# Threshold attention and a SoLU feed-forward block in one kernel: the second tile's first product moved up two rounds

## The chip, the cores and the metric

The kernel runs on one core of a Trainium2 chip. Its engines work in parallel, each through its own list of instructions in order: TensorE (PE) multiplies, VectorE (DVE), ScalarE (ACT) and GpSimd (POOL) do the elementwise work, and SyncE (SP) issues nearly all transfers. A transfer that has to wait for something is waited for by the SP queue, and what stands behind it in that queue waits too. The metric is the device time of one execution in microseconds, as the median of several.

## The reference

Attention over 8 batches of 8 heads, 576 positions, 64 elements a head, all in float32:

```
scores = q @ k.T / 8
thresh = max(scores) - tau            # per row, tau = 0.02
scores = where(scores >= thresh, scores, -1e9)
attn   = exp(scores - max(scores));  attn /= sum(attn) + 1e-9
x      = attn @ v                     # then (B, H, S, D) -> (B*S, H*D): 4608 x 512
h      = x @ w_in                     # 512 x 1024
s      = h * softmax(h)
ln     = (s - mean(s)) / sqrt(var(s) + 1e-6) * g_ln
out    = ln @ w_out                   # 1024 x 512
```

The weights `w_in` and `w_out` come as 64-bit floats, and the kernel turns them into 32-bit ones itself.

## The kernel before

**Rounds.** The attention is cut into 144 slots, 18 to a batch, and the main loop (L893) runs one slot a round. A slot is one block of 128 query rows for two heads: `scores` (L457) multiplies q by k into two PSUM tiles, `maxes` (L490) takes the row maximum on VectorE, `ramp` and `exps` (L514, L521) do threshold and exponential on ScalarE, `normalise` (L529) scales the rows on GpSimd one round later, and `blocks` (L539) turns the result into `T` on VectorE. After every second slot `blocks` also issues three transfers (L556, L558; four at L563 for the odd slots of the last rows), which move `T` into `wT`. There are two `wT` buffers, so a unit's transfer may start only when the unit two before it has been multiplied by v.

**Product with v.** `attend_steps` (L567) multiplies `wT` by v, and `attended` (L600) copies the result to `xh`, the input of the feed-forward block. When a unit is due (`pv_due`, L807), it is multiplied in the first round whose other work allows it: before the change in a round with no feed-forward step or with an h step, not beside an o step (L976).

**Feed-forward.** A tile is 128 tokens. Its product with `w_in` is two steps, h0 and h1 (L633), its product with `w_out` two steps, o0 and o1 (L751), one step a round. Between them, with h1 in round r: maximum and exponential at the end of r, product with h in r+1, statistics in r+2, normalisation on ScalarE and VectorE and the transfer `ff_swap` (L731) in r+3, the transpose `ff_turn` (L741) to `uT` at the end of r+4, and o0 can read `uT` in r+5. The variable `quarter` counts h0, h1, o0, o1; the o steps between h1 and the next h0 are those of the tile before. For the first tile there is none before, so rounds 13 and 14 have no feed-forward step (L1006 does nothing).

**Transposes and weights in the early rounds.** The q and k of the second batch are transposed on TensorE beside the scores of rounds 13 to 21 (`preps`, L813); one of these pieces, `e_item` (L413), transposes the last 64 positions of q and k, which `load_ends` (L140) brings in behind the main loads of round 9 (k) and round 11 (q). In rounds 0 to 15 each round also converts one piece of the weights (L277 to L334). Later batches are transposed on VectorE (`turn_natural`, L210), scaled on GpSimd (L197).

**SP's order.** In a round SP gets `ff_swap` first (middle jobs), then the `wT` transfers, then the store of a finished tile, then the transfers of transposed q and k, then loads (`load_at`), then those of the weights. All transfers of SP share eight completion semaphores in turn.

Work on TensorE by round, besides scores in each; "t" counts transposed pieces of q and k, a unit in brackets is (batch, kind, head pair), a tile (batch, kind, half). Starts are those of the first matmul of a round in the trace of before.

```
round  start us   before                             after
12      72.5      h1(000) v(0,1,0)                   the same
13      80.8      -                                  t5 h0(001)
14      84.6      t5                                 t4 h1(001) v(0,1,1)
15      90.8      t7 h0(001) v(0,1,1)                -
16     100.6      t6 h1(001) v(0,1,2)                t5 v(0,1,2)
17     108.8      o0(000)                            t4 o0(000)
18     113.3      o1(000)                            o1(000) v(0,1,3)
19     117.7      t5 v(0,1,3)                        t5 h0(010)
20     122.9      t7 h0(010)                         t7 h1(010)
21     128.3      t6 h1(010) v(0,2,0)                t6 o0(001)
22     135.3      o0(001)                            o1(001)
23     141.8      o1(001)                            h0(011) v(0,2,0)
24     146.2      h0(011) v(1,0,0)                   h1(011) v(1,0,0)
25     152.6      h1(011) v(1,0,1)                   o0(010)
26     158.9      o0(010)                            o1(010)
27     163.4      o1(010)                            v(1,0,1)
28     167.8      v(1,0,2)                           v(1,0,2)
29     170.7      v(1,0,3)                           v(1,0,3)
30     174.2      h0(100)                            h0(100)
```

From round 30 to the end, both kernels do the same in the same rounds, with the two PSUM buffers p0 and p1 exchanged.

Of the kernel before, what the change touches and what calls it, by code (L numbers as in the profile page):

```python
# [8 lines left out]
F32 = mybir.dt.float32  # L9
# [7 lines left out]
P = 128  # L17
# [3 lines left out]
def kernel(  # L21
# [29 lines left out]
    DM, DFF = w_in.shape  # L51
# [13 lines left out]
    work = ctx.enter_context(tc.tile_pool(name="work", bufs=2))  # L65
# [35 lines left out]
    pairs_free = ["p0", "p1"]  # L101
# [6 lines left out]
    def fence(first):  # L108
        m = nc.gpsimd.memset(mark, 0.0)
        for mm in first:  # L110
            sync(m, mm)
        return m
# [37 lines left out]
    def load_v(b, hf, parts=(0, 1, 2)):  # L150
        d = halves.setdefault((b, hf), {})
        hs = slice(4 * hf, 4 * hf + 4)

        if b > 1:
            if 0 in parts:
                d["v"] = loads.tile([P, 4, NK, D], F32, tag="v", bufs=3, name="v")
            to = d["v"].rearrange("p h m d -> p h (m d)")
            rows = v_rows[64 * (H * b + 4 * hf) :][0:256]
            for part in parts:
                nc.sync.dma_start(**(  # L160
                    dict(
                        out=to.rearrange("p (e o) n -> p o e n", o=2)[:, 0],
                        in_=rows.rearrange("(e r) n -> r e n", e=2),
                    ),
                    dict(out=to[:, 1], in_=rows[64:192]),
                    dict(out=to[ROWS[1], 3], in_=rows[0:64]),
                    dict(out=to[ROWS[0], 3], in_=rows[192:256]),
                )[part])
            return
        if 0 in parts:  # L170
            d["v"] = loads.tile([P, 4, NK, D], F32, tag="v", bufs=3, name="v")
        rest = v[b, hs, 0:SM, :].rearrange("h (p t) d -> p h (t d)", t=4)
        for part, to, rows, of in (
            (0, 0, slice(0, P), slice(0, P)), (1, 4, ROWS[0], ROWS[1]), (1, 4, ROWS[1], ROWS[0])
        ):
            if part in parts:
                nc.sync.dma_start(
                    out=d["v"][rows, :, to : to + 4].rearrange("p h t d -> p h (t d)"),
                    in_=rest[of],
                )  # L180
        for rows in ROWS if 2 in parts else ():
            nc.sync.dma_start(
                out=d["v"][rows, :, NK - 1], in_=v[b, hs, SM:S, :].rearrange("h p d -> p h d")
            )
# [7 lines left out]
    def load_natural(i, nm, a):  # L192
        raw = loads.tile([P, 4, 4, D], F32, tag=nm, name=nm)
        natural[i, nm, a] = raw = raw.rearrange("p h t d -> p (h t d)")[:, 0 : NK * D]
        nc.sync.dma_start(out=raw, in_=qk_rows[nm][a, 64 * i : 64 * i + P])
# [437 lines left out]
    def ff_h(t, part, split, beside=()):  # L633
# [29 lines left out]
        if part == 0:  # L663
            d["fence"] = fence(last[-4:])

    def ff_max(t):
        d = ffn[t]
        d["nm"] = small.tile([P, 1], F32, tag="hm", name="hm")
        nc.vector.tensor_reduce(out=d["nm"], in_=d["h"], axis=AX.X, op=ALU.max, negate=True)  # L669

    def ff_exp(t):
        d = ffn[t]

        starts.append(t)
        tag = "xh1" if rnd > NS and len(starts) % 2 else "u"
        d["u"] = work.tile([P, DFF], F32, tag=tag, bufs=1, name="u")
        d["se"] = small.tile([P, 1], F32, tag="se", name="se")
        nc.scalar.activation(  # L678
            out=d["u"], in_=d["h"], func=AF.Exp, bias=d["nm"], scale=1.0, accum_out=d["se"]
        )  # L680
# [34 lines left out]
    def ff_norm(t):  # L715
        d = ffn[t]
        rs, nb = d["norm"]
        d["V"] = V = work.tile([P, 2, DFF // 2], F32, tag="V", bufs=1, name="V")
        u = d["u"].rearrange("p (g n) -> p g n", g=2)
        nc.scalar.activation(out=V, in_=u, func=AF.Identity, bias=nb, scale=rs)  # L720

# [19 lines left out]
    def ff_turn(t, rnd):  # L741
        d = ffn[t]
        turns.append(t)
        tag = "xh0" if rnd > NS and len(turns) % 2 else "uT"
        d["uT"] = uT = work.tile([P, 2 * NC, 2, 32], F32, tag=tag, bufs=1, name="uT")
        nc.vector.transpose(  # L746
            out=uT, in_=d["V"].rearrange("p y (m x) -> p m y x", x=32)
        )
        d["turned"] = rnd + 1
# [50 lines left out]
    NS = len(slots)  # L800
    PER = NS // B
# [12 lines left out]
    for i in range(NP, 2 * NP):  # L814
        at = (13, 15, 19, 20)[i - NP]
# [7 lines left out]
    load_at = {}  # L823
    scale_at, turn_at, ends_at = {}, {}, {}
    for at, job, hf, what in (
        (11, load_one, 0, "q"),
        (9, load_one, 0, "k"),
        (13, load_one, 1, "k"),
        (15, load_one, 1, "q"),
        (17, load_v, 0, (0,)),  # L830
        (19, load_v, 0, (1, 2)),
        (PER + 3, load_v, 1, (0,)),
        (PER + 5, load_v, 1, (1, 2)),
    ):
        load_at.setdefault(at, []).append(lambda job=job, hf=hf, what=what: job(1, hf, what))
    for i in range(2 * NP, NPAIR, 2):
        b, hf = divmod(i // 2, 2)
        ats = ((-5, -3), (-1, 1)) if hf else ((-13, -11), (-9, -7))
        if b == 2:
            ats = ((-3, -2), (-1, 1)) if hf else ((-13, -11), (-9, -5))  # L840
        for nm, pieces_at in zip("qk", ats):
            for a, at in enumerate(pieces_at):
                at += PER * b
                load_at.setdefault(at - 3 if b == 2 else (at - 3) // 4 * 4, []).append(
                    lambda i=i, nm=nm, a=a: load_natural(i, nm, a)
                )
                turn_at[at] = i, nm, a
                if nm == "q":
                    scale_at[at - 1] = i, a
        for j in range(2):  # L850
            ends_at[PER * b + ats[0][1] + 4 + j] = i + j
        if hf:
            v_ats = (2, 5, 5, 6) if b % 2 else (3, 4, 4, 7)
        elif b == 2:
            v_ats = -9, -7, -5, -3
        else:
            v_ats = (-11, -7, -3, -3) if b % 2 else (-9, -5, -1, -1)
        for part, at in enumerate(v_ats):
            load_at.setdefault(PER * b + at, []).append(
                lambda b=b, hf=hf, part=part: load_v(b, hf, (part,))  # L860
            )

    with tc.manual_schedule():
# [20 lines left out]
        ready = []  # L884
        rnd = 0
        prev = cur = None

        between, starts, turns = [], [], []
        quarter = 0
        w2_done = False  # L890

        begin, middle, late, norms = {}, {}, {}, {}
        while True:  # L893
# [8 lines left out]
            if rnd in norms:  # L902
                ff_norm(norms.pop(rnd))
            if rnd == NS:
                pairs_free += ["s0", "s1"]
                if prev is not None:
                    between.append(prev)
                    prev = None
                if quarter == 2:
                    between.append(cur)  # L910
                    cur = None
                    quarter = 0
                assert quarter != 3
            if (
                cur is None and quarter == 0 and ready and ready[0][0] <= rnd
                and (more or len(between) < 3 + (len(ready[0][1][0]) == 1))
            ):
                cur = ready[0][1].pop(0)
                if not ready[0][1]:
                    ready.pop(0)  # L920
            busy = cur is not None or prev is not None
            items = []
            if rnd - 1 in pieces:
# [37 lines left out]
            due = bool(pv_due) and pv_due[0][0] <= rnd  # L961
            step = None
            if quarter < 2 and cur is not None:
                step = ("h", quarter)
            elif quarter == 3:
                step = ("o", 1)
            elif not more:
                if between and ffn[between[0]].get("turned", NS + rnd) <= rnd:
                    prev = between.pop(0)
                    step = ("o", 0)  # L970
            elif quarter == 2 or (prev is not None and not due):
                if prev is None or (ffn[prev].get("turned", NS + rnd) <= rnd and w2_done):
                    step = ("o", 0)

            attending = None
            if due and (step is None or step[0] == "h") and len(pairs_free) > (step == ("h", 0)):  # L976
                attending = pv_due.pop(0)[1]
            beside = ()
            if attending is not None and attending[1] == 2 and step is not None:
# [1 line left out]
            if step == ("h", 0):  # L981
                ff_h(cur, 0, rnd + 1 < NS, beside)
                quarter = 1
            elif step == ("h", 1):
                ff_h(cur, 1, None, beside)
                quarter = 2
                late.setdefault(rnd, []).append(lambda t=cur: (ff_max(t), ff_exp(t)))
                late.setdefault(rnd + 1, []).append(lambda t=cur: (ff_mul(t), ff_sum(t)))
                middle.setdefault(rnd + 2, []).append(lambda t=cur: ff_stats(t))
                if rnd + 6 < NS:  # L990
                    norms[rnd + 3] = cur
                else:
                    late.setdefault(rnd + 2, []).append(lambda t=cur: ff_norm(t))
                middle.setdefault(rnd + 3, []).append(lambda t=cur: (ff_norm2(t), ff_swap(t)))

                at = rnd + 4 if more or not ready or len(ready[0][1][0]) == 1 else rnd + 6
# [4 lines left out]
                if not more:  # L1001
                    between.append(cur)
                    cur = None
                    quarter = 0
            elif step == ("o", 0):
                if prev is not None:  # L1006
                    ff_o(prev, 0)
                quarter = 3
            elif step == ("o", 1):
# [5 lines left out]
                prev, cur = cur, None  # L1015
                quarter = 0
            if attending is not None:
# [3 lines left out]
                b, kind, hp = attending  # L1021
# [25 lines left out]
            if rnd - 1 in pieces:  # L1047
                weight_d(pieces[rnd - 1])
                w2_done = pieces[rnd - 1] == NW - 1
# [34 lines left out]
```

## Time and profile before

| | before |
|---|---|
| median of three runs | 866.25 us (864.14 to 867.25) |
| profiled execution, its own time | 866.93 us |
| span of its trace | 865.1 us |
| TensorE busy | 820.7 us (95%) |
| VectorE busy | 682.1 us (79%) |
| ScalarE busy | 574.1 us (66%) |
| GpSimd busy | 497.0 us (57%) |
| round 13 to the start of round 30 | 80.8 to 174.2 us |

The own time of the profiled execution is 1.8 us over its span, and 0.7 us over the median. The table of slices in the profile cuts the span into 40 stretches of 21.6 us and gives each engine's busy share in tenths. A wait is put down to the instruction whose signal came last. "L479" is line 479 of the kernel before; in the kernel after, lines behind the first edit stand a few lines lower.

### The profile page before, as it was taken

Reading aid. Unit: us, or ns where it says so; the run is one execution under the profiler, and the core shown is the slowest. Engines: PE = TensorE matmul, PEld = TensorE weight load, DVE = VectorE, ACT = ScalarE, POOL = GpSimd, SP = SyncE. Lnnn points to the kernel's source line nnn. Section 1 sums busy time; section 2 is a strip of 40 time slices with the busy share of each in tenths; the row PEclk is TensorE's granted clock in tenths of the full one; section 3 lists DMA queues with packets and bytes.
Section 4 is the critical chain, followed back from the end, with each engine's and each line's share of the span. In section 5 each row is a group of like instructions: output and inputs, shape, how many; then the busy total and the mean of one; then the engine's idle time right before and its main releaser. Section 6 shows DMA issues by size and latency. Waiting matters only on the chain.

```text
span 865.1 us, 36118 instructions
## 1 busy us (share of the span) xinstructions
PE 820.7 (95%) x15361; PEld 626.8 (72%) x15361; DVE 682.1 (79%) x1248; ACT 574.1 (66%) x1153; POOL 497.0 (57%) x938
## 2 busy tenths in 40 slices
PE   5667899999999999999999999999999999999997
PEld 3345576776688887777788886777788888887655
DVE  5989778888788878888878887888888888787361
ACT  5867776676667776777677776777677776776121
POOL 2867656657656656565656656565666655555120
PEclk9879899999999999999999999999999999999999
DMA  7999978888879888888888787888788887655312
GB/s 234 254 242 252 231 167 210 210 234 205 224 174 227 210 184 214 213 213 206 197 210 228 199 191 195 219 220 208 188 224 228 196 195 184 153 142 140 69 38 62
DMA packets 83712, 168.54 MB, mean 195 GB/s; under 512 B 15448, under 2 KB 45152, under 8 KB 83552
## 3 DMA queue, kind: packets, MB, share of 16 engines
q1 hardware_dynamic: 82416, 164.25, 76.9%
q8 instruction: 120, 1.97, 1.0%
q10 hardware_dynamic: 1136, 2.00, 0.7%
q14 instruction: 40, 0.33, 0.1%
HBM read 46.14 MB, written 9.44 MB: 64 GB/s over the span
## 4 chain that ended last, share of the span: by engine, by line
PE 82%; DMA 6%; ACT 4%; DVE 3%; issue 2%; POOL 2%; SPq 1%; ACTq 0%; DVEq 0%; POOLq 0%
PE o_ps L759 26%; PE h_ps L654 22%; PE s_ps L479 15%; PE pv L589 14%; PE h_ps L644 3%; DMA wT<-T 2%; ACT w L516 1%; DVE w L501 1%; DMA raw<-in_moe_w_out_dram 1%; ACT w L525 1%; DMA q<-in_q_dram 1%; DMA raw<-in_moe_w_in_dram 1%; DVE T L547 1%; PE s_ps L344 1%; POOL w L535 1%
## 5 line engine op out<-in xcount | busy, mean ns | idle before, releaser
L759 PE MATMUL o_ps<-w,uT 64*64 64x256 f32 x4608 | 272.3, 376 | 2.6 <-issue 2.6
L516 ACT ACTIVATE w<-s_ps,nth 128x576 f32<-128x576 f32 x280 | 196.9, 739 | 103.1 <-DVE nth L501 87.7
L501 DVE CUSTOM_DVE_ANT_0 w<-s_ps,tau_t 128x576 f32<-128x576 f32 x280 | 200.0, 751 | 82.1 <-PE s_ps L479 57.1
L759 PEld LDWEIGHTS o_ps<-w,uT 64*64 64x64 f32 x4608 | 222.8, 133 | 55.3 <-ACT xh L621 10.9
L535 POOL TENSOR_SCALAR w<-w,sm 128x576 f32<-128x576 f32 x288 | 220.7, 778 | 14.3
L547 DVE STREAM_TRANSPOSE T<-w 128x576 f32<-128x576 f32 x288 | 207.5, 755 | 22.1 <-POOL w L535 20.5
L654 PE MATMUL h_ps<-w,xh 64*64 64x512 f32 x1856 | 224.0, 590 | 0.4 <-issue 0.4
L525 ACT ACTIVATE w<-w,ntau 128x576 f32<-128x576 f32 x288 | 219.6, 767 | 0.0
L589 PEld LDWEIGHTS pv<-wT,v 64*64 64x64 f32 x5760 | 175.9, 135 | 38.5 <-issue 18.5
L479 PE MATMUL s_ps<-kT,qT 64*64 64x64 f32 (+1 forms) x2048 | 180.9, 422 | 14.0 <-ACT w L516 12.4
L589 PE MATMUL pv<-wT,v 64*64 64x128 f32 (+1 forms) x5760 | 176.8, 262 | 7.6 <-DMA wT<-T 4.9
L654 PEld LDWEIGHTS h_ps<-w,xh 64*64 64x64 f32 x1856 | 124.1, 133 | 72.5 <-issue 31.6
L532 POOL TENSOR_SCALAR sm<-sm 128x2 f32<-128x2 f32 x144 | 36.0, 250 | 198.9 <-ACT w L525 195.6
L533 POOL TENSOR_TENSOR sm<-sm,mone 128x2 f32<-128x2 f32 x144 | 108.3, 752 | 12.0
L479 PEld LDWEIGHTS s_ps<-kT,qT 64*64 64x64 f32 x2048 | 75.2, 139 | 23.3 <-ACT w L516 18.4
L621 ACT COPY xh<-pv 128x256 f32<-128x256 f32 x64 | 24.9, 390 | 75.7 <-PE pv L589 75.7
L720 ACT ACTIVATE V<-u,nb,rs 128x1024 f32<-128x1024 f32 x36 | 44.7, 1241 | 42.0 <-POOL nb L710 35.1
L746 DVE STREAM_TRANSPOSE uT<-V 128x1024 f32<-128x1024 f32 x36 | 44.3, 1230 | 16.6 <-DMA V<-u 16.3
L525 ACT ACTIVATION_READ_ACCUMULATOR w<-w,ntau 128x1 f32 x288 | 55.6, 193 | 0.0
L684 DVE TENSOR_TENSOR u<-h_ps,u 128x1024 f32<-128x1024 f32 x36 | 42.8, 1189 | 9.8 <-ACT u L678 9.8
L725 DVE TENSOR_SCALAR u<-u,rs,nb 128x1024 f32<-128x1024 f32 x36 | 34.9, 971 | 17.6 <-ACT V L720 17.6
L669 DVE TENSOR_REDUCE hm<-h_ps 128x1 f32<-128x1024 f32 x36 | 42.9, 1192 | 5.9 <-PE h_ps L654 3.1
(90 smaller groups left out, 575.7 us busy)
## 6 DMA issues: line engine op xcount, KB each, us to landing
wT<-T SPq DMA_DIRECT2D x160, 288.0 KB, 6.4
wT<-T SPq DMA_DIRECT2D x64, 576.0 KB, 5.8
V<-u SPq DMA_DIRECT2D x144, 64.0 KB, 3.5
out_dram<-ob SPq DMA_DIRECT2D x71, 128.0 KB, 2.7
q<-in_q_dram SPq DMA_DIRECT2D x24, 288.0 KB, 6.2
qT<-flip SPq DMA_DIRECT2D x48, 144.0 KB, 3.9
k<-in_k_dram SPq DMA_DIRECT2D x24, 288.0 KB, 5.8
kT<-flip SPq DMA_DIRECT2D x48, 144.0 KB, 4.2
```

The source lines that it names most:

```text
L479: nc.tensor.matmul(out=ps[h][ROWS[y], ks], lhsT=lhsT, rhs=d["kT"][ROWS[h], ks], start=True, stop=True,)
L501: nc.vector.tensor_tensor_reduce(out=w, in0=ps[:, 0:S], in1=(zero if loose else tau_t).to_broadcast([P, S]), scale=1.0, scalar=BIG, op0=AL ...
L516: nc.scalar.activation(out=d["w"][x], in_=d["w"][x] if d["loose"] else d["ps"][x][:, 0:S], func=AF.Prelu, bias=d["nth"][x], scale=-1.0, al ...
L525: nc.scalar.activation(out=w, in_=w, func=AF.Exp, bias=ntau, scale=1.0, accum_out=sm[:, x : x + 1])
L533: nc.gpsimd.tensor_tensor(out=sm, in0=sm, in1=mone, op=ALU.pow)
L535: nc.gpsimd.tensor_scalar(out=w, in0=w, scalar1=sm[:, x : x + 1], scalar2=1.0, op0=ALU.mult, op1=ALU.mult)
L547: nc.vector.transpose(out=T[:, :, r, h, :], in_=w)
L589: nc.tensor.matmul(out=to, lhsT=d["v"][ROWS[u], (h0 + h - u) % 4 if b > 1 else h0 + h, m ^ 4 * u if m < 8 and b < 2 else m,], rhs=rhs, sta ...
L654: mm = nc.tensor.matmul(out=h[ROWS[y], f], lhsT=x[ROWS[r], c, ROWS[y]], rhs=w1_parts[ROWS[r], c, part ^ r], start=part == 0 and c == 0, st ...
L720: nc.scalar.activation(out=V, in_=u, func=AF.Identity, bias=nb, scale=rs)
L746: nc.vector.transpose(out=uT, in_=d["V"].rearrange("p y (m x) -> p m y x", x=32))
L759: nc.tensor.matmul(out=d["o"][ROWS[z], 512 * (r ^ other) : 512 * (r ^ other) + 256], lhsT=d["uT"][ROWS[r], m].rearrange("p y x -> p (y x)" ...
```

## The change

Six edits. `SECOND` names tile (0,0,1). Its u, V and uT get tiles of the tags xh3 and xh2, which are free in those rounds, in place of the buffers that the first tile still uses. The loop takes a second tile at once when the first has no predecessor whose o steps would stand between (`quarter == 2 and prev is None`), so that h0 and h1 of the second tile are done in rounds 13 and 14. A due product with v may also stand beside an o step in round 18 (`rnd == PER`). And the loads of v for the second half of batch 1 go from rounds 21 and 23 to 24 and 25, those of the second q and first k of batch 2 from rounds 22 and 24 to 21 and 23.

```diff
+    SECOND = (0, 0, 1)
...
-        tag = "xh1" if rnd > NS and len(starts) % 2 else "u"
+        tag = "xh1" if rnd > NS and len(starts) % 2 else "xh3" if t == SECOND else "u"
...
-        d["V"] = V = work.tile([P, 2, DFF // 2], F32, tag="V", bufs=1, name="V")
+        tag = "xh2" if t == SECOND else "V"
+        d["V"] = V = work.tile([P, 2, DFF // 2], F32, tag=tag, bufs=1, name="V")
...
-        tag = "xh0" if rnd > NS and len(turns) % 2 else "uT"
+        tag = "xh0" if rnd > NS and len(turns) % 2 else "xh3" if t == SECOND else "uT"
...
-        (PER + 3, load_v, 1, (0,)),
-        (PER + 5, load_v, 1, (1, 2)),
+        (PER + 6, load_v, 1, (0,)),
+        (PER + 7, load_v, 1, (1, 2)),
...
-                load_at.setdefault(at - 3 if b == 2 else (at - 3) // 4 * 4, []).append(
+                if b == 2:
+                    of = at - 3 - (at in (PER + 7, PER + 9))
+                else:
+                    of = (at - 3) // 4 * 4
+                load_at.setdefault(of, []).append(
...
+            if quarter == 2 and prev is None and ready and ready[0][0] <= rnd and not w2_done:
+                prev, cur = cur, ready[0][1].pop(0)
+                if not ready[0][1]:
+                    ready.pop(0)
+                quarter = 0
...
-            if due and (step is None or step[0] == "h") and len(pairs_free) > (step == ("h", 0)):
+            if (
+                due and (step is None or step[0] == "h" or rnd == PER)
+                and len(pairs_free) > (step == ("h", 0))
+            ):
```

## The prediction

> **What bounds the kernel now.** I read the windows first, to see where TensorE is not the bound:
>
> ```profile
> 80.80:100.60 19.80, 14.12 (x260) 8.85 (x253) 17.73 (x35) 16.11 (x36) 12.97 (x20) 0.83 1.07 247
> 174.20:186.50 12.30, 11.61 (x174) 6.75 (x174) 10.05 (x19) 9.59 (x22) 8.57 (x17) 1.00 0.82 218
> 186.50:210.00 23.50, 23.01 (x424) 16.56 (x418) 18.64 (x35) 15.33 (x31) 13.68 (x26) 1.00 0.87 212
> 210.00:790.00 580.00, 577.46 (x11084) 464.66 (x11080) 481.10 (x872) 404.89 (x801) 350.86 (x681) 1.00 0.81 200
> ```
>
> After the length come busy times of PE, PE's weight load, DVE, ACT and POOL, then the granted TensorE clock and the DMA share. From 186.5 to 790 us TensorE works 600.5 of 603.5 us: what rounds 13 to 30 gain or lose arrives at the end nearly whole. In 80.8 to 100.6 us (rounds 13 to 15) it works 14.1 of 19.8, at a clock of 0.83, while DVE works 17.7 and the DMA engines are full. The timeline of TensorE there:
>
> ```profile
> 80.89 1.23 PE L479 MATMUL s_ps<-kT,qT 64*64 64x512 f32 x12
> 84.58 0.33 PE L344 MATMUL s_ps<-ident,k 64*64 64x64 f32 x4 [2.46 <-ACT w L516]
> 85.21 1.12 PE L344 MATMUL s_ps<-ident,k 64*64 64x64 f32 x28 [0.30 <-ACT w L516]
> 86.26 0.49 PE L344 MATMUL s_ps<-ident,ends 64*64 64x64 f32 x8
> 86.53 2.09 PE L479 MATMUL s_ps<-kT,qT 64*64 64x64 f32 x16
> ```
>
> The waits are for the ramp that frees the score tiles; more follow in round 15 (2.18 and 0.75). After them scores take 2.09 instead of the 1.35 of later rounds. The line with "ends" matters: what it reads was issued here (transfers of that moment, then SP's timeline later):
>
> ```profile
> ends<-in_q_dram SPq DMA_DIRECT2D x1, 128.0 KB, 9.8
> ...
> 139.44 0.58 SPq L556 DMA_DIRECT2D wT<-T  x1
> 140.07 2.98 SPq L558 DMA_DIRECT2D wT<-T  x2
> ...
> wT<-T SPq DMA_DIRECT2D x2, 288.0 KB, 5.8
> ...
> 151.89 3.58 SPq L736 DMA_DIRECT2D V<-u  x4
> 155.59 0.63 SPq L556 DMA_DIRECT2D wT<-T  x1
> ```
>
> SP issued that load at 76.40 us, so it landed at 86.2, just as round 14 used it. Of one wT set, the two L558 transfers take 2.98 us to issue and land 5.8 us after theirs. Lastly DVE's timeline, where the transpose to uT waits for the V transfer, and SP's longest waits:
>
> ```profile
> 157.00 1.25 DVE L746 STREAM_TRANSPOSE uT<-V 128x1024 f32<-128x1024 f32 x1 [0.46 <-DMA V<-u]
> ...
> SPq L563 <- DVE T L547: 7.6, 1, 7.6
> ```
>
> From the first V issue to the transpose are 5.1 us.
>
> **What the Trainium skill says.** "TensorE: Matmul & The Clock Gate", Part 1: after an idle window the array runs at half rate until it has been busy for about 3.4 us. The trace agrees in kind (clock 0.83, scores 2.09 against 1.35). "DMA: Bandwidth & Descriptors", Anatomy of one DMA: the wait for a semaphore happens on the issuing sequencer, before dispatch. The trace agrees: SP stood 7.6 us for DVE at 118.75, and nothing moved in the meantime. So a transfer that waits holds all later ones.
>
> **The change part by part.** Matrix work is the same in sum. Prices from steady rounds of this trace: scores 1.0, h or o step 3.43, product with v 1.95, a transposed piece 0.115 us.
>
> Round 13. Its transposes now stand ahead of its scores, and e_item reads the load that lands at 86.2. TensorE, free at 81.0, waits some 5 us; the scores end at 88.6, cold, as round 14's did before. Behind them waits DVE: its next work is round 13's maxima, at 88.66, where before it had round 14's.
>
> From there DVE has no gap. Durations of before: two maxima 1.4, T 1.4, product with h 1.1, weight piece 1.25 and 0.7, statistics 1.4, maximum of h 1.1, normalisation 0.75. Round 13 (maxima, T, product, weights) 5.8; round 14 (maxima, statistics, T, maximum, weights) 7.2; round 15 (maxima, normalisation, T, product, last weight) 5.9: to 107.5. TensorE does h0 to 92.4, h1 to 97.4, v(0,1,1) to 99.3, scores of 15 to 100.3. The maxima of 15 start at 101.6, and ACT, which has the first tile's V (1.15) ahead of its ramps, is done with them at 105.0. TensorE has been idle 4 us; round 16's transposes and scores take 3.4, as in round 14 before, to 108.4. DVE: maxima 1.4, statistics 1.4, T 1.4, uT 1.1: 113.8. o0 of the first tile starts there (before: 109.86), round 17 ends at 117.3, round 18 (1.0 + 3.43 + 1.95) at 123.7, and five transposes and scores of round 19 at 125.3. Before, as much was done at 122.87. **+2.4 us.** Without the wait in round 13 I get R18's end at 119.7 in place of 123.7: -1.6, which is what the filled rounds are worth.
>
> From 122.87 to round 28 (167.78) before took 44.9 for 42.9 of work (13 transposes, eight scores, four h, four o, three v); the rest is mainly 1.7 us in o0 of round 22 that the trace puts down to no one. I don't carry it over: **-2.0.** Bounds: it comes again, 0.
>
> Round 22 to 25. v(0,2,0) moves from round 21 to 23, as 21 and 22 are o steps now. wT of (1,0,1), issued in round 22, needs that buffer. SP stands until the end of round 23, 6.5 us after its start (scores, h and 2.1 of product). Behind it: V of tile (0,1,0), two stores, q and k of batch 2. Issuing wT takes 3.6 (139.44 to 143.05), then V needs 5.1 to the transpose, 1.2 for it: uT at 16.4 us from round 23's start. o0 in round 25 could start at 13.8 (6.4 each for rounds 23 and 24, 1.0 for scores). **+2.5**; bounds 0.5 (V passes wT quickly) and 4.
>
> Rounds 26 to 29. v(1,0,1) moves from 25 to 27, and wT of (1,0,3), issued in 26, needs its buffer. Third transfer issued 2.1 after the first, landing 5.8 later: 8 us after v(1,0,1) ends. Until then TensorE has scores, v(1,0,2), scores: 4.4 with DVE's pace in 28 (0.4 later than before). v(1,0,3) waits **+3.6**, and the 0.4 counts too. Bounds 2.5 and 5. Since h0 of round 30 reads this product, nothing else can go ahead. Behind wT on SP stand V of (0,1,1), a store, k's halves and v of batch 2; V is needed only in round 30, and is landed by then.
>
> Round 30 and after: before lost 0.35 twice in rounds 30 and 31 to waits for maxima and ramp; TensorE now comes later than they: **-0.7.**
>
> The edits with no price: the buffers of SECOND (the same size, the weights' raw pieces in them are read by round 15, V comes in 17, u at the end of 14 in the one read by 13); the product in 18, counted above; v(0,1,3) is there in time, as T is made at 112.7 and the transfers land in 8 us or a little more. The moved loads: v is needed in 28 and lands, behind wT of (1,0,2), about 2 us ahead; if not, round 28 waits that long. k is turned in 27, q in 23 and 25.
>
> Sum: 2.4 - 2.0 + 2.5 + 0.4 + 3.6 - 0.7 = +6.2 us on the span of 865.1 (own time 866.93, the median 0.7 below it). **Forecast 872.5 us**, 0.7% slower.
>
> **Rivals.**
> A. The loads land early. If the ends of q land by 81.4 in place of 86.2, round 13 does not wait, the early rounds give -1.6 in place of +2.4, and the end is 868.5: no change that counts. Each us of landing before 86.2 gives about 0.8. For it: SP's order up to there is the same, and a landing varies (7.8 for the other ends load). Against: the DMA engines are full, and the load before took 9.8.
> B. The two wT waits are hidden, as a free DMA lands faster. If a wT set lands within 4 us of its release, both terms go (-6.1) and the time is 866.5, no change; with A too, 862.5, faster. Against: 5.8 us for a third transfer alone, with a busy share of 0.9 or so.
> C. VectorE stays the bound after round 17, or v of batch 1 is late in 28 as well: another 3 to 5 us, 876 to 877. For it: DVE works 10.3 of 10.8 us in rounds 27 to 29 before.
> That the edit does nothing is excluded: the order of the instructions shows h of (0,0,1) moved.
>
> **How the numbers follow.** 0.3% is 2.6 us, about what a measurement of this kernel tells from no change. Forecast 0.60; A 0.12, B 0.10 (0.04 of it with A), C 0.18. Slower: forecast, C and a third of A, 0.82; same: the rest of A and most of B, 0.13; faster 0.05. Range: lower end with A's half and the low bound of one wT wait, 867.0; upper, with C, 877.
>
> **What would show it.** Right: in round 13 TensorE waits about 5 us for the ends of q; DVE has no gap from round 13 to 16; SP stands some 6 us in round 22 for v(0,2,0), uT of (0,1,0) waits for V; v(1,0,3) waits 3 to 4 us for wT. Round 30 then starts at about 180 instead of 174.2. Wrong: round 13's scores done by 83, or no wait of v(1,0,3) for wT, or a new wait after round 31, where I expect the two traces to be the same.

## The result, and the profile after

The kernel after takes 876.76 us (870.98 to 878.8, six executions) where the kernel before takes 864.91 (862.67 to 867.25, six): a ratio of 1.0123, 95% interval 1.0092 to 1.0154. A second series of the same kernel gave 875.93 (1.0116, 1.008 to 1.0151), so it is about 10 us slower. The forecast was 872.5 with a range up to 877: the sign and the range are right, the middle was some 4 us too low. As a difference, 6.2 us were forecast and 10 to 12 came.

The profiled execution happened to be the fastest of its six, 870.98 us with a span of 869.2. Its trace therefore shows a loss of 4.1 us in the span, not 10 to 12. Its waits are the same in kind as in a second profiled execution, which is shown with the experiments.

The windows of the kernel after, for rounds 13 to 15 up to the first transposes of 16, rounds 30 and 31, and the long rest (columns as before: length, busy time of PE, weight load, DVE, ACT and POOL, granted clock, DMA share, GB/s):

```profile
77.15:101.74 24.59, 16.07 (x268) 7.47 (x261) 16.57 (x34) 16.08 (x35) 13.79 (x21) 0.86 0.85 204
180.74:194.36 13.62, 11.48 (x179) 7.27 (x175) 8.42 (x16) 8.13 (x18) 9.22 (x18) 1.00 0.94 257
210.00:790.00 580.00, 578.79 (x11132) 473.97 (x11126) 483.03 (x872) 405.28 (x803) 350.64 (x680) 1.00 0.81 202
```

The early stretch is no denser than before: TensorE works 16.1 of 24.6 us. From 210 us on it works without a break, as before, so what is lost was lost before that. Where, is told by the timeline of TensorE, cut to the lines with a wait behind them (start, duration, what ran, and in brackets the idle time ahead of it with its releaser):

```profile
82.83 0.49 PE L344 MATMUL s_ps<-ident,ends 64*64 64x64 f32 x8 [4.85 <-DMA ends<-in_q_dram]
101.74 0.34 PE L344 MATMUL s_ps<-ident,k 64*64 64x64 f32 x4 [3.68 <-ACT w L516]
...
159.10 5.37 PE L762 MATMUL o_ps<-w,uT 64*64 64x256 f32 x64 [3.49 <-DVE uT L749]
173.39 2.18 PE L589 MATMUL pv<-wT,v 64*64 64x128 f32 x68 [0.36 <-DMA v<-in_v_dram]
...
178.93 2.07 PE L589 MATMUL pv<-wT,v 64*64 64x128 f32 x66 [0.66 <-DMA wT<-T]
...
192.55 2.07 PE L589 MATMUL pv<-wT,v 64*64 64x128 f32 x66 [1.51 <-DMA wT<-T]
```

In order: round 13 waits 4.85 us for the ends of q; round 16 waits 3.68 for a ramp; o0 of round 25 waits 3.49 for `uT`, and then takes 5.37 us (the o step after it takes 3.66); v(1,0,3) in round 29 waits only 0.66 (0.26 more ahead of it); v(1,1,0) in round 31 waits 1.51 (0.63 ahead of it). What is behind the wait of round 25 stands in SP's timeline, SP's longest wait for a product (in all, times, longest), and DVE's timeline:

```profile
148.31 0.58 SPq L556 DMA_DIRECT2D wT<-T  x1
148.93 2.92 SPq L558 DMA_DIRECT2D wT<-T  x2
151.95 4.17 SPq L739 DMA_DIRECT2D V<-u  x4
```

```profile
SPq L556 <- PE pv L589: 7.9, 2, 5.8
```

```profile
157.71 1.25 DVE L749 STREAM_TRANSPOSE uT<-V 128x1024 f32<-128x1024 f32 x1 [5.80 <-DMA V<-u]
```

SP stands 5.8 us for the product v(0,2,0), which reads the buffer that the new `wT` is to go into. Only then are `wT` (from 148.31) and, behind it, V of tile (0,1,0) issued. VectorE stands 5.80 us for V, and TensorE for VectorE. The idle time also costs TensorE its clock: the windows give 0.68 for that o step.

```profile
159.10:164.40 5.30, 5.29 (x73) 4.19 (x77) 5.30 (x9) 3.97 (x8) 1.04 (x3) 0.68 0.97 260
```

To see where time goes I use the lag: the start of a round's scores in a kernel, minus that in the profiled execution of before. Where the order of the work differs (rounds 13 to 29), a lag also holds the difference in work done; from round 30 on it does not. In the profile of after: round 12 -3.6, round 13 +2.3, round 23 -0.3, round 26 +5.3, round 30 +6.5, round 32 +7.9, round 42 +4.5, and then about 4.1 to the end. The early rounds were luck: up to round 12 both kernels do the same, and after was 3.6 us ahead there. All of that is gone in round 13, since it waits for a transfer.

The fall from +7.9 to +4.5 between rounds 32 and 42 is not the change's doing either. The one trace of before, from which all lags are taken, lost 3.4 us there: its rounds 34, 35, 40 and 41 took 6.80, 7.31, 7.21 and 5.65 us, those of after 6.37, 6.37, 6.38 and 4.43. A kernel that does the same as before in these rounds (the control below) is 2.6 us faster in them, too. What the change costs is therefore better read from round 12 to round 32: 11.5 us in this trace, 7.8 in the second one, and the times say 10 to 12.

### The profile page after: what moved, and what is told of

Same layout as the page of the kernel before. It is cut to its first block, busy times and chain, and to the rows that moved or that the text cites. A ratio compares the mean times of both kernels' runs of the same rounds, so it can differ in the third digit from the quotient of the medians.

```text
span 869.2 us, 36123 instructions
## 1 busy us (share of the span) xinstructions
PE 820.3 (94%) x15361; PEld 633.9 (73%) x15361; DVE 682.8 (79%) x1249; ACT 573.4 (66%) x1152; POOL 499.7 (57%) x938
## 4 chain that ended last, share of the span: by engine, by line
PE 83%; DVE 4%; DMA 4%; ACT 4%; issue 2%; SPq 2%; POOL 1%; ACTq 0%; DVEq 0%; POOLq 0%
PE o_ps L762 26%; PE h_ps L654 23%; PE s_ps L479 15%; PE pv L589 15%; PE h_ps L644 3%; DMA wT<-T 1%; ACT w L516 1%; DMA ends<-in_q_dram 1%; DVE w L501 1%; ACT w L525 1%; DVE T L547 1%; DVE w L305 1%; PE s_ps L344 1%; DMA k<-in_k_dram 1%; SPq L739 1%
## 5 line engine op out<-in xcount | busy, mean ns | idle before, releaser
L762 PEld LDWEIGHTS o_ps<-w,uT 64*64 64x64 f32 x4608 | 228.0, 134 | 53.9 <-ACT xh L621 10.2
L479 PE MATMUL s_ps<-kT,qT 64*64 64x64 f32 (+1 forms) x2048 | 177.6, 419 | 12.3 <-ACT w L516 10.9
L654 PEld LDWEIGHTS h_ps<-w,xh 64*64 64x64 f32 x1856 | 126.6, 134 | 70.0 <-issue 32.2
L532 POOL TENSOR_SCALAR sm<-sm 128x2 f32<-128x2 f32 x144 | 38.0, 264 | 190.4 <-ACT w L525 187.0
L680 ACT ACTIVATE u<-h_ps,hm 128x1024 f32<-128x1024 f32 x36 | 40.1, 1114 | 13.8 <-DVE hm L671 8.4
```

The source lines that it names most:

```text
L479: nc.tensor.matmul(out=ps[h][ROWS[y], ks], lhsT=lhsT, rhs=d["kT"][ROWS[h], ks], start=True, stop=True,)
L654: mm = nc.tensor.matmul(out=h[ROWS[y], f], lhsT=x[ROWS[r], c, ROWS[y]], rhs=w1_parts[ROWS[r], c, part ^ r], start=part == 0 and c == 0, st ...
L762: nc.tensor.matmul(out=d["o"][ROWS[z], 512 * (r ^ other) : 512 * (r ^ other) + 256], lhsT=d["uT"][ROWS[r], m].rearrange("p y x -> p (y x)" ...
```

## The experiments

All changes are against the kernel after unless it says before. Each kernel's ratio is to executions of the kernel before that were taken beside it on the same chip.

### Three suspected waits, one at a time and together

**The ends of q loaded in round 9.** They come right behind the ends of k, so round 13 should not wait.

```diff
-                load_ends(b, nm, slice(0, 2) if len(parts) > 1 else slice(0, H), queue)
+                if len(parts) > 1:
+                    load_ends(b, nm, slice(0, 2), queue)
+                elif nm == "k":
+                    load_ends(b, "k", slice(0, H), queue)
+                    load_ends(b, "q", slice(0, H), queue)
```

> The changed kernel, with the load of the ends of q issued in round 9 behind the ends of k instead of in round 11. My theory: the 4.85 us wait of TensorE for them in round 13 goes, and of it about 4 us reach the rounds behind, so the time is some 4 us under the changed kernel (0.5%). Rival, that VectorE bounds rounds 13 to 16 in any case: the wait goes and less than 1 us is won.

Measured: 871.17 us (867.25 to 872.49), 1.0065 [1.0041, 1.009]. The wait is gone, and some 5 us of the loss with it. In its place an idle time appears in h0 of the same round that the trace puts down to nothing:

```profile
84.93 3.16 PE L658 MATMUL h_ps<-w,xh 64*64 64x512 f32 x25 [1.89 <-issue]
```

**v(0,2,0) beside o1 in round 22**, so that SP's `wT` transfer finds its buffer free a round earlier; the next two units are held in the rounds that after has for them.

```diff
+    hold = {(1, 0, 0): PER + 6, (1, 0, 1): PER + 9}
+    pv_due = [(hold.get(u, at), u) for at, u in pv_due]
...
-                due and (step is None or step[0] == "h" or rnd == PER)
+                due and (step is None or step[0] == "h" or rnd in (PER, PER + 4))
```

> The changed kernel, with the product of unit (0,2,0) beside o1 in round 22 instead of beside h0 in round 23; the next units stay where the change has them. Theory: SP no longer stands in round 22, V of tile (0,1,0) lands before its transpose, the 3.49 us wait of o0 in round 25 goes, 3 to 3.5 us won there. Rival, that V is late for another cause (the transfers ahead of it): the wait of o0 stays over 2 us.

Measured: 869.19 us (865.43 to 876.61), 1.006 [1.0036, 1.0083]. SP's timeline has the `wT` transfer at 144.11 instead of 148.31, o0 of round 25 follows its scores at once, and its window shows full clock:

```profile
144.11 0.58 SPq L556 DMA_DIRECT2D wT<-T  x1
```

```profile
156.18 3.63 PE L762 MATMUL o_ps<-w,uT 64*64 64x256 f32 x64
```

```profile
156.20:159.80 3.60, 3.60 (x80) 2.60 (x76) 3.31 (x7) 3.45 (x7) 1.09 (x3) 1.00 0.97 272
```

So the stand of SP costs some 5.5 us: the two ratios differ by 0.63%, and round 25 as a whole takes 9.96 us in after and 4.43 here. Of that, 3.49 us are the wait and 1.7 the slower clock (5.37 against 3.63 for the same step).

**v(1,0,1) right behind v(1,0,0) in round 24**, so that the `wT` of (1,0,3) need not wait for round 27.

```diff
+    hold = {(1, 0, 2): PER + 10, (1, 0, 3): PER + 11}
+    pv_due = [(hold.get(u, at), u) for at, u in pv_due]
...
+            if rnd == PER + 6:
+                unit = pv_due.pop(0)[1]
+                for _ in attend_steps(unit):
+                    pass
+                attended(unit)
```

> The changed kernel, with the product of unit (1,0,1) in round 24 behind that of (1,0,0) instead of in round 27; the units behind stay in rounds 28 and 29. Theory: the transfers of wT of (1,0,3) go out in round 26 without waiting for a product, the waits of the products in rounds 29 and 31 for wT (0.9 and 2.1 us) go, and the time falls by 2 to 4 us. Rival, that these waits are only the load on the DMA engines: they stay, and the time is the same.

Measured: 875.06 us (872.14 to 880.31), 1.0121 [1.0088, 1.0153]: no gain. The timelines of DVE and of TensorE say why:

```profile
160.14 1.25 DVE L749 STREAM_TRANSPOSE uT<-V 128x1024 f32<-128x1024 f32 x1 [5.61 <-DMA V<-u]
```

```profile
173.77 0.33 PE L479 MATMUL s_ps<-kT,qT 64*64 64x64 f32 x4 [3.10 <-ACT w L516]
```

VectorE still stands 5.61 us for V. TensorE does not feel it in round 25, as round 24 is longer by a product; but round 27 has none now, and at the start of round 28 it waits 3.10 us for the ramp behind the late VectorE. The waits that the edit was aimed at do shrink, to none in round 29 and 0.99 us in round 31, but that wins nothing.

**All three together**, with the holds this needs: v(0,2,0) in round 22, (1,0,0) and (1,0,1) in 24, none in 27. The other lines are those of the three diffs above.

```diff
+    hold = {(1, 0, 0): PER + 6, (1, 0, 2): PER + 10, (1, 0, 3): PER + 11}
```

> All three at once: ends of q in round 9, (0,2,0) in round 22, (1,0,1) in round 24. Theory: the three waits account for the loss, and without them the early filling is left: 2 to 5 us under the kernel before (0.994 to 0.998 of its time). Rival, that the change costs something beyond these waits: still over the kernel before.

Measured: 868.01 us (862.91 to 875.5), 1.0035 [1.0016, 1.0054]. Still over before; after round 27 without a product TensorE waits 2.64 us for a ramp here too.

### Is it the wait, or the load?

**A control: before with the ends of q in round 9** (the first diff above).

> A control: the kernel before with the one edit of ends9, the last 64 positions of q loaded in round 9 behind those of k. Theory (that load's landing is a cost only for after, because only after reads it at the start of round 13): no change, ratio 0.998 to 1.002, since before reads it in round 14, behind a ramp that ends later. Rival (the load in round 11 disturbs others, so any kernel gains from its move): ratio 0.996 or less, and then the 0.6% that ends9 won over after is not evidence for the wait of round 13.

Measured: 865.65 us (860.58 to 873.05), 1.0003 [0.9974, 1.0032]. The edit gives the kernel before nothing, so what it gives after is the wait in round 13.

**The moved loads put back**: v, q and k in rounds 21 to 24, as in before.

```diff
-        (PER + 6, load_v, 1, (0,)),
-        (PER + 7, load_v, 1, (1, 2)),
+        (PER + 3, load_v, 1, (0,)),
+        (PER + 5, load_v, 1, (1, 2)),
...
-                    of = at - 3 - (at in (PER + 7, PER + 9))
+                    of = at - 3
```

> The kernel after with the loads of v (second half of batch 1), q and k (batch 2) in the rounds in which before has them. Theory (the moved loads have no price, as the prediction says): 875 to 878 us, ratio 1.010 to 1.015, and SP's stand of about 6 us in round 22, the wait for V and the wait for uT remain, since the wT transfer that stands there is ahead of the loads in SP's order. Rival (the loads in rounds 20 to 25 are what makes the wT transfers and V late): 3 us or more under after, ratio at most 1.008, with the waits of products with v for wT down from 5.7 us to before's 3.7.

Measured: 877.58 us (875.46 to 885.69), 1.0151 [1.0109, 1.0194]. The interval overlaps that of after, but the profile (SP's longest wait, then TensorE in round 25) shows that my text named the wrong transfer:

```profile
SPq L177 <- PE pv L589: 11.3, 1, 11.3
```

```profile
163.36 5.04 PE L762 MATMUL o_ps<-w,uT 64*64 64x256 f32 x64 [5.61 <-DVE uT L749]
```

With the loads in their old rounds it is a load of v (L177) that stands for the late product, and it stands 11.3 us, since it is issued a round before the `wT` transfer. o0 of round 25 then waits 5.61 instead of 3.49. So moving the loads takes 2 us off the wait of TensorE that the product in round 18 brings, by these two traces; in the times the two kernels are not told apart. The rival is out: with the loads back, nothing is won.

### The kernel after, once more

> The kernel after, unchanged, for more executions and a second profile: its profiled execution took 870.98 us where its median is 876.76, so what the typical one loses is not in that trace. Theory 1 (an early round that depends on when loads land): the second profile, if it lies at 874 us or more, shows the additional time before round 23 (the lag of round 13 on before is +3 or more, not +2.3), and the same waits as the first. Theory 2 (the wT transfers land late in a typical execution): the additional time is in rounds 27 to 32, with v(1,0,3) waiting 3 us or more for wT, as I had forecast for rounds 26 to 29. Median 875 to 878 either way.

Measured: 875.93 us (872.83 to 878.26), profiled span 872.7. SP's longest wait is the same:

```profile
SPq L556 <- PE pv L589: 7.9, 2, 5.8
```

Neither theory holds as written: up to round 23 the lag is that of the first profile (-0.6 after -0.3), and no product with v waits more than 1.6 us for `wT`. By round 42 it is 5.2 after 4.5. The two traces get there by different ways: this one starts round 12 at +0.7, not -3.6, and waits only 2.78 us for the ends of q in round 13, not 4.85. Another 2.2 us come between rounds 90 and 114, where both kernels do the same; TensorE's timeline has there

```profile
630.06 0.69 PE L589 MATMUL pv<-wT,v 64*64 64x64 f32 x32 [1.20 <-issue]
```

This is no work of the change: the control, which differs from before in one early load, loses 4.6 us in the same place. The lag in round 42 is free of this, the span is not. But it still holds the luck of the rounds up to 12 and the 3 us or so that the trace of before lost by round 42.

### The two halves of the change apart

**After without the product in round 18.** v(0,1,3) goes to round 19, and from there on all stands in before's rounds; only h of tile (0,0,1) is early, and the loads are moved.

```diff
-                due and (step is None or step[0] == "h" or rnd == PER)
+                due and (step is None or step[0] == "h")
```

> The kernel after without the product beside o1 in round 18: v(0,1,3) then goes to round 19 and every step and product from round 19 on stands in the same round as in the kernel before; only h of tile (0,0,1) is two rounds earlier, and the loads are apart. Theory (the loss is made of two separate parts, an early one in round 13 and a late one from round 22 on, and the late one comes from the product in 18, which moves everything up by one round): the wait for the ends of q in round 13 stays at 4 to 5 us, there is no stand of SP in round 22 for v(0,2,0), no wait of o0 for uT over 1 us, and the total is 865 to 870 us, ratio 1.000 to 1.005. Rival (what is lost comes from the early h and its wait, and the later waits only follow from being late): 873 us or more, ratio over 1.008.

Measured: 871.91 us (865.69 to 877.9), 1.0063 [1.0041, 1.0084]. Between the two expectations: SP has no long stand for a product in round 22 and `uT` is waited for 0.4 us at most, as the theory said, but the early half alone costs 0.6%, here with a wait of 3.50 us in round 13. TensorE's timeline:

```profile
86.07 0.49 PE L344 MATMUL s_ps<-ident,ends 64*64 64x64 f32 x8 [3.50 <-DMA ends<-in_q_dram]
...
143.82 3.02 PE L762 MATMUL o_ps<-w,uT 64*64 64x256 f32 x49 [1.70 <-issue]
```

The second line is the unassigned 1.7 us in o0 of round 22 that before has too. It comes back with before's order.

**The same with the ends of q in round 9** (both diffs).

> The early h alone, with its wait taken away: no product in round 18, and the ends of q loaded in round 9. Theory (filled rounds 13 and 14 are worth 1.6 us, as the prediction worked out, once no load is waited for, and from round 19 on all stands as before): 862 to 865.5 us, ratio 0.996 to 1.000. Rival (VectorE is the bound of rounds 13 to 16, so that filling TensorE there gives nothing): ratio 1.000 to 1.004.

Measured: 867.51 us (860.92 to 872.54), 1.0005 [0.9983, 1.0027]. The early half's 0.6% was the wait for the ends of q. But in this trace the early h does not win anything: the lag goes from +3.3 in round 12 to +3.4 in round 18. The interval does not separate the two expectations. As in the first experiment, h0 of round 13 loses time to nothing that the trace shows, and here it then runs at a clock of 0.69. VectorE stands 3.45 us for the scores behind it (TensorE's timeline, then DVE's):

```profile
88.02 4.86 PE L658 MATMUL h_ps<-w,xh 64*64 64x512 f32 x25 [2.08 <-issue]
```

```profile
94.19 0.76 DVE L505 CUSTOM_DVE_ANT_0 w<-s_ps,tau_t 128x576 f32<-128x576 f32 x1 [3.45 <-PE s_ps L483]
```

So what went missing in round 13 was not lost to a busy VectorE, as the rival has it. Only after that, from 94.19 to 117.94 us, does VectorE have no gap over 0.3 us, and there TensorE waits 3.57 us for a ramp ahead of round 16.

**Before with only the product beside o1 in round 18**, loads and h as they were.

```diff
-            if due and (step is None or step[0] == "h") and len(pairs_free) > (step == ("h", 0)):
+            if due and (step is None or step[0] == "h" or rnd == PER) and len(pairs_free) > (step == ("h", 0)):
```

> The other half: the kernel before with nothing but the product v(0,1,3) beside o1 in round 18. h of tile (0,0,1) stays in rounds 15 and 16, and from round 19 on every step and product stands in the round of the kernel after. Theory (two separate parts): no wait for the ends of q, but SP stands about 6 us in round 22, o0 of round 25 waits 3 us or more for uT and runs cold, the round of v(1,1,0) waits for wT, and the total is 870 to 873 us, ratio 1.005 to 1.009. Rival (the product in 18 costs only where the early part was already late): ratio 1.003 or less.

Measured: 875.28 us (871.49 to 880.62), 1.0115 [1.0073, 1.0157], more than the theory said. The transfer that stands is again a load of v, as the loads are where before has them. SP's longest wait, then TensorE in round 25:

```profile
SPq L177 <- PE pv L589: 9.6, 1, 9.6
```

```profile
160.59 6.20 PE L759 MATMUL o_ps<-w,uT 64*64 64x256 f32 x64 [5.50 <-DVE uT L746]
```

So the product in round 18 needs no early h to do its harm.

### Two tries at a version that beats both

**Nothing held back**: the ends of q in round 9, a product allowed beside o in rounds 18 and 22, every later unit of batch 1 a round earlier, v's loads where before has them. The lines for the ends of q and for v's loads are those above.

```diff
-                due and (step is None or step[0] == "h" or rnd == PER)
+                due and (step is None or step[0] == "h" or rnd in (PER, PER + 4))
```

> A version meant to beat both: the kernel after with the ends of q in round 9, the product v(0,2,0) beside o1 in round 22 and, unlike in the earlier run, nothing held back, so that each later unit of batch 1 moves up by one round and no round is left without a product; the loads of v for batch 1 at before's rounds, as v is needed a round earlier. Theory: the early rounds give -1.6, the stand in round 22 is gone, and rounds 23 to 30 lose at most 2 us to waits for wT: 863 to 867 us, ratio 0.997 to 1.002. Rival (the packed rounds pay their gain back in rounds 23 to 32 whatever the order, since the wT transfers now follow one another too closely): 868 us or more, ratio 1.003 or over, with over 5 us of waits of products with v for wT.

Measured: 880.11 us (874.76 to 883.7), 1.0166 [1.0122, 1.0209], the slowest of all. The lag is +5.6 in round 30 and +11.3 in round 42: the same stall comes again, this time for v(1,1,0), which now falls in round 33. SP's longest wait for a product is 5.2 us, and TensorE has in round 35

```profile
211.49 6.46 PE L766 MATMUL o_ps<-w,uT 64*64 64x256 f32 x64 [4.34 <-DVE uT L753]
```

**Two waits removed, nothing else moved**: the ends of q in round 9, v(0,2,0) in round 22 with the two units held; v(1,0,1) stays in round 27.

> The kernel after with two of its waits taken away, that for the ends of q (round 9) and that of SP for v(0,2,0) (beside o1 in round 22, the units behind it held as after has them); v(1,0,1) stays in round 27, unlike in the run with all three. Theory (the two gains of 0.6% each add, and moving v(1,0,1) away from round 27 only cost time): 862 to 866 us, ratio 0.996 to 1.001. Rival (the gains overlap, as what is won before round 23 is lost again in rounds 23 to 30): 868 us or more, ratio 1.003 or over.

Measured: 866.48 us (862.69 to 874.96), 1.0012 [0.9981, 1.0043]. The gains add: within the 0.3% that the interval leaves, the whole loss is gone. But nothing is won over before. Next to 3.57 us for a ramp ahead of round 16, TensorE's largest wait left is that for v in round 28:

```profile
169.68 2.07 PE L593 MATMUL pv<-wT,v 64*64 64x128 f32 x66 [2.36 <-DMA v<-in_v_dram]
```

A third `wT` buffer might take SP's stand away at its root. That was not tried.

### Put together

| kernel | ratio to before | lag in round 42, us | of it after round 12, us |
|---|---|---|---|
| before, ends of q in 9 | 1.0003 | -2.2 | -1.5 |
| early h, ends of q in 9 | 1.0005 | 2.0 | -1.3 |
| after, ends of q in 9, v(0,2,0) in 22 | 1.0012 | -0.4 | 0.8 |
| after with all three edits | 1.0035 | 2.5 | 2.2 |
| after, v(0,2,0) in 22 | 1.006 | 0.2 | 1.1 |
| early h | 1.0063 | 2.5 | -0.4 |
| after, ends of q in 9 | 1.0065 | 4.0 | 5.2 |
| after | 1.0123, 1.0116 | 4.5, 5.2 | 8.1, 4.5 |
| product in 18 only, old loads | 1.0115 | 6.4 | 6.7 |
| after, v(1,0,1) in 24 | 1.0121 | 7.2 | 6.2 |
| after, old loads | 1.0151 | 7.8 | 9.4 |
| after, nothing held back | 1.0166 | 11.3 | 12.3 |

The ends of q cost 0.58% with the product in 18 (1.0123 to 1.0065), 0.48% once v(0,2,0) is in 22 (1.006 to 1.0012), and 0.58% without the product (1.0063 to 1.0005). SP's stand costs 0.63% (1.0123 to 1.006) or 0.53% (1.0065 to 1.0012). Each of these differences is uncertain by 0.3 to 0.4%, by the intervals of the kernels it is taken from; that they agree, and that both edits together bring the time back to before's, is what carries the reading: two separate losses of about 5 us each, and together the whole of it. In the last column the first row, the control, is the zero; "early h" has the moved loads.

## Why the prediction was right, and where it was off

**The wait in round 13: right.** 4.85 us against "some 5" (2.78 in the second trace). The landing was at 82.8, not 86.2, but SP had issued that load at 73.11 instead of 76.40 and TensorE was early by nearly as much. I had +2.4 with the wait and -1.6 without, so 4.0 for it; the three pairs above give 4 to 5.

**"-1.6 is what the filled rounds are worth": too large, and not seen in the times.** From the first matmul of round 13 to the first scores of round 17, with the same work done, before takes 28.0 us. Four kernels with h early and the ends of q in round 9 take 26.8 to 27.2, so they win 0.8 to 1.2 us; the fifth, which has no product in round 18, takes 28.4. Its time shows no gain, 1.0005 with an interval of some 2 us to each side. VectorE was in the sum, without a gap from 88.66 on; in the trace of after it has gaps of 0.7 at most from 85.28 to round 16, so that part was nearly right. What the sum does not have is the idle time in h0 of round 13, 1.7 to 2.1 us in four of these five kernels. That it makes up the shortfall is not shown: the kernel with only 0.48 us of it wins no more than the others.

**-2.0 not carried over: right.** The idle 1.7 us in o0 of round 22 is not in after, and is there again, at the same matmul, in the three kernels that have before's order in those rounds (early h 1.70, with the ends of q in 9 0.61, the control 1.32). Why that order brings it no trace tells.

**SP's stand in round 22: right in mechanism, too small.** The stand is 5.8 us (6.5 expected), V and `uT` are late by it, o0 of round 25 waits 3.49 against +2.5. What I missed is the clock: the page of the Trainium skill that I had cited, "TensorE: Matmul & The Clock Gate", Part 1, says that an idle window halves the rate for some microseconds, and I applied it to round 13 only. Here the clock is 0.68 and o0 takes 5.37 us against 3.63 at full clock. With these 1.7 us the term comes to 5.2, above its upper bound of 4; with the edit undone the ratios give 4.6 to 5.5 for it.

**v(1,0,3) behind `wT` in round 29: wrong, 0.9 us instead of 3.6.** v(1,0,1) ends at about 171.6 and the bulk of the product starts at 178.9, 7.3 us later, nearly as worked out (8). But TensorE was not there waiting: it came to the product only 6 us after v(1,0,1), not 4.4. Round 28 took 4.06 us, not the 3 of its work, with 0.36 of wait for v, and round 29 lost another 0.35 to VectorE's maxima. Small delays ahead of a wait run beside it and are taken off it; they don't add to it. The other half of that step, +0.4 for round 28, is in those figures.

**-0.7 after round 30: right there, and then a wait that I had excluded.** Round 30 takes 4.41 us against 5.27 before, so 0.86 comes back. In round 31 v(1,1,0) waits 2.1 us for `wT`, the lag goes from 5.7 to 7.9. I had written that the traces are the same from round 31 on; their work is, but the transfers in flight are not. The 3.4 us that come back between rounds 32 and 42 were lost by the trace of before.

**The moved loads, "no price": off.** They save 2 us of the wait in round 25, by the traces.

**A reading of the trace of before that is too strong.** While SP stood 7.6 us up to 118.75, no new transfer went out, but those under way still moved: the DMA share is 0.53 over that stretch and 0.23 over its last 4.7 us. That the transfers behind a waiting one wait too does not depend on it.

**The rivals.** A (the ends of q land early) did not happen. Of B one of the two waits did go, that of round 29, but not because the DMA was faster: the set took 7.3 us, and TensorE came later. C had the time, 876 to 877, by another cause: v in round 28 was late by only 0.36. Neither profiled execution, at 871.0 and 874.5, is a typical one: the median over all twelve is 876.7, and what the others lost besides no trace here tells.

**What was luck.** That the range held is in part luck: the wait in round 29 that was too large, the stall in round 25 that was too small and the wait in round 31 that was not foreseen made up for one another, and the upper end had been set for a cause that hardly acted. By the prediction's own signs, v(1,0,3) should have waited 3 to 4 us and no new wait should have come from round 31 on. Round 30 starts at 180.7, as forecast (180), but only because this execution was 3.6 us ahead in round 12.

## What to carry to other kernels

When a schedule packs a consumer into a later round, ask of each transfer whose buffer it frees, and then what stands behind that transfer in the queue: here a product two rounds later held a `wT` transfer for 5.8 us, and it was the unrelated V behind it that stopped TensorE. Price a stall of TensorE with the slow work after it (here 3.5 us of wait and another 1.7). And before filling an idle engine, look whether the next engine has room: beside a VectorE with hardly a gap, two rounds filled on TensorE were worth some 1 us in four of five traces, and nothing that the times show.

## What was not expected of the hardware

"DMA: Bandwidth & Descriptors" of the Trainium skill, Anatomy of one DMA, has the wait on the issuing sequencer; the traces agree, and show how far it reaches: one load of v that stood 11.3 us delayed a transfer for another engine and, through it, TensorE by 5.6. Where a load had been waited for (4.85 us), taking the wait away brought out an idle time of 1.7 to 2.1 us in the next step, in four kernels of five, that the trace puts down to nothing. It needs no such edit: before with only the product in round 18 has 1.92 us of it in h0 of round 16. And the same instructions, far from any change, take up to 4.6 us more between rounds 90 and 114 than in the trace of before, in some kernels' traces and not in others.
